# First block's projection of a two-block MLP kernel: seven products of quarters of x in chunks 1 to 3

## The chip, the core and the metric

The kernel runs on one core of a Trainium2 chip. The metric is the device time of one execution in microseconds (us), lower is better. PE is the matrix engine, DVE the vector engine, ACT the scalar engine, POOL the GpSimd engine; SP issues DMAs. The engines run at once, each working off its own queue in order, and wait for one another on semaphores.

## What is computed

Two batches of 576 tokens with 8 heads of 64 go through attention with a relative bias; the result x (1152 tokens by 512 features) goes through two blocks:

```python
h = x @ w_in                              # 512 -> 2048
g = h * clip(h + 3, 0, 6) / 6
x = g @ w_out                             # 2048 -> 512
a, b = x @ w_a, x @ w_b                   # 512 -> 1536 each
out = (a * b) @ w_out2                    # 1536 -> 512
```

The change lies in the first of these five lines and in the hand-over to the third.

## The kernel before

All matrices lie with features on the 128 partitions and tokens along the free axis. Every value is held in two parts of a shorter format, a high part (rounded) and a low part (the rest), and every product of two matrices is made as three matmuls: high by high, high by low, low by high. So each tensor that PE reads costs ACT a cast (the high part) and DVE a subtraction (the low part).

The **first block** runs in four chunks of 512 of the 2048 hidden features (`FC` = 4 tiles of 128). A chunk has two stages:

- Projection: `hidden(w, i, blk)` for 4 tiles i by 3 token blocks of 384. `proj` makes 12 matmuls (4 tiles of the 512 input features, three each) into one bank of PSUM; ACT makes relu(h+3) (L620), DVE min(.,6)*h (L621). `split_g` (L612, L613) puts the high and low parts into gh[i] and gl[i].
- Output: `out1(ch, c, w, blk)` for 4 output tiles c by 3 token blocks, 12 matmuls each over the four gh/gl, with sums over the chunks in `part` (L668 on ACT in chunk 0, L670 on DVE after).

Three pairs of PSUM banks take the groups of matmuls in turn (`bank`). In the last chunk `last_out1` weaves the first sums of the second block in between. The **second block** already uses Winograd's form of Strassen's seven products: the weight of a unit is cut into 2 by 2 quarters (A11, A12, A21, A22 with the sums S1 to S4), x into 2 by 2 quarters (two halves of the features, two halves of 576 tokens; B11, B21, B22 with the sums T1 to T4). `product` (L804) makes 12 matmuls of 288 columns for one product of one output tile, in one pair of banks; two output tiles share the weights.

**Weights** come in packed form, 68 pieces of 128x512 (`_Weights`). A piece k is loaded (three buffers `raw`, SP), `rebias` on ACT (L1014) and `join` on DVE (q = 0: L1023, q = 1: nothing, q = 2: L1027, which frees the buffer and issues the next load) restore it; `split` casts it to a slot on ACT (L1043) and takes the low part on POOL (L1044). Pieces of a unit of quarters are combined on POOL first (`combine`, L1050). `tick` and `tock` emit these steps, some joins and one slot step, between the groups of matmuls. Low parts of g wait in `later` until the next tick. The order in which the program emits the instructions is the order in each engine's queue; no scheduler changes it.

The first groups of chunk 0 are mixed with the end of the attention (L625 to L641). Then PE goes through chunk 0's output, and chunks 1, 2 and 3.

## Time and profile before

| | before |
|---|---|
| time, median of 3 runs (lowest to highest) | 583.74 us (583.36 to 584.54) |
| the profiled execution's own time | 584.19 us |
| its span | 582.4 us |
| PE / DVE / ACT / POOL busy in the span | 569.7 / 400.7 / 334.6 / 243.1 us |
| attention (PE at the first block alone from here on) | 0 to 175.1 us |
| first block, chunk 0: output from 193.9; chunks 1, 2, 3 from | 218.9, 268.9, 318.9 us |
| second block | 368.9 us to the end |

The span runs from the first to the last instruction of the profiled execution. Busy time of an engine counts the time in which at least one instruction runs. The matmul durations of the trace are longer than their spacing, since they overlap: what a stretch of PE costs is read from starts, not from durations. "Granted clock" 1.00 is PE's full 2.4 GHz; it is 1.00 in every stretch used here.

### The profile page before, as it was taken

Reading aid. Unit: us, or ns where it says so; the run is one execution under the profiler, and the core shown is the slowest. Engines: PE = TensorE matmul, PEld = TensorE weight load, DVE = VectorE, ACT = ScalarE, POOL = GpSimd, SP = SyncE. Lnnn points to the kernel's source line nnn. Section 1 sums busy time; section 2 is a strip of 40 time slices with the busy share of each in tenths; the row PEclk is TensorE's granted clock in tenths of the full one; section 3 lists DMA queues with packets and bytes.
Section 4 is the critical chain, followed back from the end, with each engine's and each line's share of the span. In section 5 each row is a group of like instructions: output and inputs, shape, how many; then the busy total and the mean of one; then the engine's idle time right before and its main releaser. Section 6 shows DMA issues by size and latency. Waiting matters only on the chain.

```text
span 582.4 us, 13871 instructions
## 1 busy us (share of the span) xinstructions
PE 569.7 (98%) x5580; PEld 508.9 (87%) x5580; DVE 400.7 (69%) x809; ACT 334.6 (57%) x661; POOL 243.1 (42%) x259
## 2 busy tenths in 40 slices
PE   8899999999999999999999999999999999999997
PEld 5267776777789999999999999999889998899986
DVE  6999999988968725865764657856752649637352
ACT  6899999987667646633640653554455543345310
POOL 0086566556844312221121532463446834367200
PEclk9999999999999999999999999999999999999999
DMA  7796877478524532443342201011271122500012
GB/s 253 225 345 165 271 215 227 117 223 191 122 66 154 166 126 73 144 145 108 110 144 73 73 0 37 1 38 43 86 248 59 37 73 72 181 2 2 1 72 92
DMA packets 29505, 69.60 MB, mean 120 GB/s; under 512 B 5888, under 2 KB 6272, under 8 KB 29440
## 3 DMA queue, kind: packets, MB, share of 16 engines
q1 hardware_dynamic: 29296, 68.61, 38.6%
q8 instruction: 44, 0.72, 0.6%
q14 instruction: 21, 0.17, 0.1%
q10 hardware_dynamic: 144, 0.09, 0.1%
HBM read 55.44 MB, written 13.25 MB: 118 GB/s over the span
## 4 chain that ended last, share of the span: by engine, by line
PE 79%; issue 7%; DVE 4%; DMA 4%; ACT 3%; POOL 1%; SPq 1%; DVEq 0%; ACTq 0%; POOLq 0%
PE pair L595 47%; PE pair L804 22%; PE sc L306 3%; PE pvb L403 3%; DMA scr<-E 2%; PE tp L347 2%; PE bps L225 2%; ACT P L323 2%; DMA bias<-scr 2%; DVE P L319 1%; DVE ht L200 1%; SPq L273 1%; PE pvb L399 1%; DMA raw<-in_wm_dram 1%; ACT PT L383 1%
## 5 line engine op out<-in xcount | busy, mean ns | idle before, releaser
L1044 POOL TENSOR_TENSOR slot<-wv,slot 128x512 fp32r<-128x512 f32 x86 | 119.5, 1395 | 219.4 <-ACT slot L1043 153.5
L595 PE MATMUL pair<-xx,slot 128*128 128x384 f32 x576 | 101.5, 335 | 0.0
L595 PEld LDWEIGHTS pair<-xx,slot 128*128 128x128 f32 x576 | 99.8, 188 | 0.2
L595 PE MATMUL pair<-gh,slot 128*128 128x384 f32 x384 | 98.6, 336 | 0.0
L804 PE MATMUL pair<-xx,slot 128*128 128x288 f32 x576 | 83.3, 296 | 0.3 <-DVE c L838 0.3
L804 PEld LDWEIGHTS pair<-xx,slot 128*128 128x128 f32 x576 | 78.6, 188 | 1.1 <-DVE c L838 0.6
L595 PEld LDWEIGHTS pair<-gh,slot 128*128 128x128 f32 x384 | 69.5, 188 | 0.0
L595 PE MATMUL pair<-slot,gh 128*128 128x512 f32 (+1 forms) x224 | 68.0, 386 | 0.0
L341 POOL TENSOR_SCALAR P<-P,st 128x576 f32<-128x576 f32 x72 | 54.7, 772 | 30.6 <-DVE st L336 14.7
L1014 ACT ACTIVATE wv<-raw 128x512 f32<-128x512 f32 x68 | 45.6, 671 | 37.6 <-DMA raw<-in_wm_dram 25.2
L595 PE MATMUL pair<-gl,slot 128*128 128x384 f32 x192 | 64.4, 336 | 0.0
L323 ACT ACTIVATE P<-P,st 128x576 f32<-128x576 f32 x72 | 55.9, 778 | 13.7 <-DVE st L319 13.3
L804 PE MATMUL pair<-tt,slot 128*128 128x288 f32 x432 | 63.5, 296 | 0.0
L1043 ACT CAST slot<-wv 128x512 fp32r<-128x512 f32 x86 | 53.1, 621 | 14.1 <-PE pair L804 6.1
L804 PEld LDWEIGHTS pair<-tt,slot 128*128 128x128 f32 x432 | 59.3, 188 | 0.2 <-ACT u L887 0.2
L620 ACT ACTIVATE t<-pair,three 128x384 f32<-128x384 f32 x48 | 28.0, 582 | 49.7 <-PE pair L595 49.7
L200 DVE TENSOR_SCALAR ht<-cs,scl,negb 128x576 f32<-128x576 f32 (+17 forms) x107 | 54.1, 543 | 0.0
L319 DVE CUSTOM_DVE_ANT_0 P<-sc,bias 128x576 f32<-128x576 f32 x72 | 51.5, 749 | 2.6 <-DMA bias<-scr 1.4
L1023 DVE TENSOR_SCALAR wm<-wv 128x512 uint32<-128x512 uint32 x59 | 40.5, 687 | 18.4 <-ACT wv L1014 18.4
L621 DVE SCALAR_TENSOR_TENSOR u<-t,pair 128x384 f32<-128x384 f32 x48 | 26.6, 554 | 38.2 <-ACT t L620 38.2
L595 PEld LDWEIGHTS pair<-slot,gh 128*128 128x128 f32 x224 | 41.4, 188 | 8.7
L595 PE MATMUL pair<-slot,gl 128*128 128x512 f32 (+1 forms) x112 | 43.0, 384 | 0.0
(118 smaller groups left out, 928.6 us busy)
## 6 DMA issues: line engine op xcount, KB each, us to landing
raw<-in_wm_dram SPq DMA_DIRECT2D x68, 512.0 KB, 3.5
scr<-E SPq DMA_DIRECT2D x36, 295.5 KB, 4.5
bias<-scr SPq DMA_DIRECT2D x17, 288.0 KB, 4.5
bias<-scr SPq DMA_DIRECT2D x17, 256.0 KB, 4.7
kraw<-in_kt_dram SPq DMA_DIRECT2D x8, 288.0 KB, 4.5
qraw<-in_qm_dram SPq DMA_DIRECT2D x8, 256.0 KB, 3.8
VM<-in_vm_dram SPq DMA_DIRECT2D x2, 1024.0 KB, 7.3
out_dram<-part SPq DMA_DIRECT2D x7, 256.0 KB, 2.0
```

The lines of the kernel that those rows point to most:

```text
L200: V.tensor_scalar(ht[:, :Dd], ltab[:, :Dd], scalar1=sc, scalar2=negb, op0=ALU.mult, op1=ALU.max)
L319: V.tensor_tensor_reduce(out=Pu, in0=sc[:, :, 0:288], in1=bt, scale=-0.125, scalar=3.0e38, op0=ALU.add, op1=ALU.min, accum_out=st[:, u : u ...
L323: A.activation(P[:, u, :], P[:, u, :], AF.Exp, bias=st[:, u : u + 1], scale=-1.0, accum_out=st[:, 2 + u : 3 + u])
L341: G.tensor_scalar(P[:, u, :], P[:, u, :], scalar1=st[:, 2 + u : 3 + u], scalar2=1.0, op0=ALU.mult, op1=ALU.mult)
L595: T.matmul(ps_ap, l, r, start=(i == 0), stop=(i == len(prods) - 1))
L620: A.activation(t, hp, AF.Relu, bias=three[:, 0:1])
L621: V.scalar_tensor_tensor(out=u, in0=t, scalar=6.0, in1=hp, op0=ALU.min, op1=ALU.mult)
L804: T.matmul(pair[:, j, 0:TQ], l, r, start=start and i == 0, stop=i == 5, skip_group_check=not start)
L1014: self.nc.scalar.activation(self.u[k], up, AF.Prelu, scale=2.0**-112, alpha=-(2.0**32))
L1023: V.tensor_scalar(mid, ub, scalar1=3, scalar2=0xFFFFFFFF, op0=ALU.logical_shift_left, op1=ALU.bitwise_and)
L1043: nc.scalar.copy(s[:, 0, :], v)
L1044: nc.gpsimd.tensor_tensor(out=s[:, 1, :], in0=v, in1=s[:, 0, :].bitcast(F32), op=ALU.subtract)
```

## The change

The projection of chunks 1 to 3 is made in quarters, as in the second block. `seven_products(ch)` replaces the twelve calls of `hidden` of a chunk: a unit is the whole chunk (its 4 tiles are two output tiles m = 0, 1 by two halves), so it has 7 products for each m, 14 in all, of 12 matmuls with 288 columns. The four pieces of weights of such a chunk are packed as quarters (last part of the diff), and POOL makes S1 to S4 from them.

The quarters B11, B21, B22 of x are parts of x itself; T1 to T4 are made once, in steps (`x_sums`, `x_steps`): one step behind each `hidden` and each `out1` of chunk 0. T2 to T4 lie in `tt`, T1 takes the place of the quarter B12 in x when chunk 0 no longer needs it. In all this is 22 instructions on DVE, 4 on POOL and 8 on ACT, all of 576 columns.

A chunk's projection then has, on DVE, 7 additions of a product and a kept sum, 8 gates (L921) and 8 low parts (L878), and on ACT 6 copies out of PSUM, 8 relus (L918) and 8 casts. The output stage of chunks 1 to 3 begins with `out1_two`: token blocks 0 and 1 of the first two output tiles run in pairs, and the tile of gh/gl that is finished last is multiplied last. In every `out1` the low part gl is now used after the two matmuls with gh. In `join_next`, `rebias(k + 1)` is emitted one step later, with the empty step q = 1.

```diff
...
+SEVEN = 1
...
+    def x_steps():
+        for _ in range(min(xrate[0], len(xsteps))):
+            xsteps.pop(0)()
...
         split_g(u, i, blk)
+        x_steps()
...
+    def x_parts(name, src, c):
+        def part(h):
+            return seven[name][h][:, c]
+
+        return (
+            lambda: A.copy(part(0), src),
+            lambda: V.tensor_tensor(out=part(1), in0=src, in1=part(0).bitcast(F32), op=ALU.subtract),
+        )
...
+    def x_sums():
+
+        def two(eng, out, a, b, op):
+            return lambda: eng.tensor_tensor(out=out, in0=a, in1=b, op=op)
+
+        minus, plus = ALU.subtract, ALU.add
+        steps = []
+        for c in range(2):
+            (h11, l11), (h12, l12), (h21, l21), (h22, l22) = (
+                [x_of(x, h, k, c).bitcast(F32) for x in (xh, xl)] for h in range(2) for k in range(2)
+            )
+            t1 = xt1[:, c]
+            (hi2, lo2), (hi3, lo3), (hi4, lo4) = (
+                x_parts(n, x, c) for n, x in (("T2", xt2), ("T3", xt3), ("T4", xt4))
+            )
+            eng = V if c else G
+            t3 = [two(eng, xt3, xt2, h11, minus), two(eng, xt3, xt3, l11, minus)]
+            t4 = [two(eng, xt4, h21, xt2, minus), two(eng, xt4, xt4, l21, plus)]
+            sums = [
+                two(V, t1, h12, h11, minus),
+                two(V, t1, t1, l12, plus),
+                two(V, t1, t1, l11, minus),
+                two(V, xt2, h22, t1, minus),
+                two(V, xt2, xt2, l22, plus),
+            ]
+            if c == 0:
+                steps += [[f] for f in sums]
+                steps[4] += t3
+                steps += [[hi2], [lo2] + t4]
+                kept = [[hi3], [lo3], [hi4], [lo4]]
+            else:
+                steps += [[f] + k for f, k in zip(sums, kept + [[]])]
+                steps += [[t3[0], hi2], [t3[1], lo2], [t4[0], hi3], [t4[1], lo3], [hi4], [lo4]]
+        for ops in steps:
+            xsteps.append(lambda ops=ops: [f() for f in ops])
...
+    seven.update({
+        "B11": (xh[:, 0:2, 0:TH], xl[:, 0:2, 0:TH]),
+        "T1": (xh[:, 0:2, TH:NTOK], xl[:, 0:2, TH:NTOK]),
+        "B21": (xh[:, 2:4, 0:TH], xl[:, 2:4, 0:TH]),
+        "B22": (xh[:, 2:4, TH:NTOK], xl[:, 2:4, TH:NTOK]),
+    })
+    for i, name in enumerate(("T2", "T3", "T4")):
+        seven[name] = (tt[:, 0, i], tt[:, 1, i])
...
-            pr += [(wh, gh[i][:, blk, :]), (wh, gl[i][:, blk, :]), (wl, gh[i][:, blk, :])]
+            pr += [(wh, gh[i][:, blk, :]), (wl, gh[i][:, blk, :]), (wh, gl[i][:, blk, :])]
...
+    def out1_two(ch, c0, ws, blk, last):
+
+        accs = [bank()[:, :TB] for _ in ws]
+        prs = [out1_products(w, blk) for w in ws]
+        seq = [0, 1, 5 - last, last]
+        for part in (seq[:2], seq[2:3], seq[3:]):
+            for acc, pr in zip(accs, prs):
+                for f in part:
+                    for i in range(3 * f, 3 * f + 3):
+                        T.matmul(acc, *pr[i], start=i == 0, stop=f == last and i == 3 * f + 2, skip_group_check=True)
+        for j, acc in enumerate(accs):
+            out1_sum(ch, c0[j], blk, acc)
+        for _ in ws:
+            tick(2)
...
+        x_steps()
...
-        for j, blk in ((0, 0), (1, 0), (0, 1), (0, 2), (1, 1), (1, 2)):
+        out1_two(ch, (0, 2), ws, 1, 2)
+        later.append(split("B11", quarter(0, 0, 0), 0))
+        for j, blk in ((0, 2), (1, 2)):
             out1(ch, 2 * j, ws[j], blk)
-            if (j, blk) == (0, 1):
-                later.append(split("B11", quarter(0, 0, 0), 0))
-            elif blk == 2 or (j, blk) == (1, 1):
+            for _ in range(1 + j):
                 next(half)
...
+    def first_gate(q, i0, c):
+        t = pw3.tile([128, 2, TQ], F32, tag="h", bufs=3, name="ht")
+        A.activation(t, c, AF.Relu, bias=three[:, 0:1])
+
+        def gate():
+            V.scalar_tensor_tensor(out=t, in0=t, scalar=6.0, in1=c, op0=ALU.min, op1=ALU.mult)
+            split_q(t, q, i0)
+
+        gates.append(gate)
+
+    def run_gate():
+        gates.pop(0)()
+        hi, lo = halves.pop(0)
+        hi()
+        later.append(lo)
+
...
+    def seven_products(ch):
+        quarters[0] = seven
+        X, X2, Y = oldest()
+        slots = {}
+
+        def use(pair, m, a, b, start):
+            if a not in slots:
+                slots[a] = ring.take((2 * FC * ch, a))
+            product(pair, slots[a], m, b, start)
+            if m == 1:
+                ring.free(slots[a])
+
+        def beat():
+
+            run_lo(len(later))
+            for _ in range(len(gates)):
+                run_gate()
+            ring.work(1, 1)
+
+        use(X, 0, "A11", "B11", True)
+        A.copy(s1, X[:, :, 0:TQ])
+        beat()
+        use(X2, 0, "S1", "T1", True)
+        beat()
+        use(X, 0, "S2", "T2", False)
+        A.copy(u2, X[:, :, 0:TQ])
+        beat()
+        use(Y, 0, "A12", "B21", True)
+        quarter_out("11", 0, 0, Y, s1)
+        use(X, 0, "S3", "T3", False)
+        A.copy(u3, X[:, :, 0:TQ])
+        beat()
+        use(Y, 1, "A11", "B11", True)
+        quarter_out("22", 0, 0, X2, u3)
+        A.copy(s1, Y[:, :, 0:TQ])
+        use(X, 0, "A22", "T4", False)
+        beat()
+        quarter_out("21", 0, 0, X, None)
+        use(X2, 0, "S4", "B22", False)
+        X, X2, Y = Y, X, X2
+        use(X, 1, "S2", "T2", False)
+        quarter_out("12", 0, 0, Y, u2)
+        run_lo(len(later))
+        A.copy(u2, X[:, :, 0:TQ])
+        run_gate()
+        ring.work(0, 1)
+        run_gate()
+        use(Y, 1, "A12", "B21", True)
+        use(X2, 1, "S1", "T1", True)
+        quarter_out("11", 1, 2, Y, s1)
+        run_lo(len(later))
+        A.copy(s1, X2[:, :, 0:TQ])
+        run_gate()
+        use(X, 1, "S3", "T3", False)
+        ring.work(0, 1)
+        c22 = pw2.tile([128, 2, TQ], F32, tag="c", bufs=3, name="c")
+        V.tensor_tensor(out=c22, in0=X[:, :, 0:TQ], in1=s1, op=ALU.add)
+        A.copy(u3, X[:, :, 0:TQ])
+        first_gate("22", 2, c22)
+        run_lo()
+        use(Y, 1, "A22", "T4", True)
+        quarter_out("21", 1, 2, Y, u3)
+        run_gate()
+        use(X2, 1, "S4", "B22", False)
+        run_gate()
+        quarter_out("12", 1, 2, X2, u2)
+        later.reverse()
+        run_lo(2)
+        run_gate()
+        order[:] = [X, Y, X2]
+        turn[0] = -1
...
+            if ch == SEVEN - 1:
+                t1_parts = [x_parts("T1", xt1[:, c], c) for c in range(2)]
+                xsteps[:] = xsteps + [part for hi_lo in zip(*t1_parts) for part in hi_lo]
+                xrate[0] = XR
+        else:
+            if ch == SEVEN:
+                while xsteps:
+                    xsteps.pop(0)()
+                for f in later:
+                    f()
+                later.clear()
+                pt1.release()
+                pt.release()
+                pw2 = tc.alloc_tile_pool(name="pw2", bufs=1, side="left", reuse_waits="tile")
+                s1, u2, u3 = (pw2.tile([128, 2, TQ], F32, name=n) for n in ("s1", "u2", "u3"))
+                pw3 = tc.alloc_tile_pool(name="pw3", bufs=1, side="left", reuse_waits="tile")
+            seven_products(ch)
...
+        for c in range(0, NC, 2):
+            ws = [ring.take(), ring.take()]
+            if ch >= SEVEN and c == 0:
+                out1_two(ch, (0, 1), ws, 0, 3)
+                out1_two(ch, (0, 1), ws, 1, 2)
+            for blk in range(2 if ch >= SEVEN and c == 0 else 0, 3):
+                for j in range(2):
+                    out1(ch, c + j, ws[j], blk, 2 if ch >= SEVEN else None)
+            ring.done(2)
...
-        if q == 0:
+        if q == 1:
             self.rebias(k + 1)
...
-        pieces += [wi[f] for f in range(f0, f0 + FC)]
+        if f0 < FC * SEVEN:
+            pieces += [wi[f] for f in range(f0, f0 + FC)]
+        else:
+            for df, h in ((0, 0), (1, 0), (1, 1), (0, 1)):
+                pieces.append(np.concatenate([wi[f + df][:, 256 * h : 256 * h + 256] for f in (f0, f0 + 2)], axis=1))
         pieces += [rows(moe_w_out, f0, c) for c in (range(NC) if f0 + FC < NF1 else (0, 2, 1, 3))]
...
```

In the order of PE's queue, at the projection of chunk 1 (xx is x with its high and low parts, tt holds T2 to T4, pair is PSUM, slot the weights), the first rows before:

```order
L595 MATMUL pair_3558<-xx,slot_2832 128x384 x12
L595 MATMUL pair_3821<-xx,slot_2832 128x384 x12
L595 MATMUL pair_3557<-xx,slot_2832 128x384 x12
L595 MATMUL pair_3558<-xx,slot_2833 128x384 x12
L595 MATMUL pair_3821<-xx,slot_2833 128x384 x12
```

and of the change:

```order
L866 MATMUL pair_3558<-xx,slot_2832 128x288 x12
L866 MATMUL pair_3830<-xx,slot_2833 128x288 x12
L866 MATMUL pair_3558<-tt,slot_2835 128x288 x12
L866 MATMUL pair_3557<-xx,slot_2834 128x288 x12
L866 MATMUL pair_3558<-tt,slot_2836 128x288 x12
```

Twelve groups of 12 matmuls with 384 columns became fourteen groups of 12 with 288.

On DVE, at the end of the projection of chunk 2 and the start of its output, in the change (c is an addition, ht a gate, gl a low part, part a sum of the output; gl_3568 and gl_3569 are tiles 2 and 3):

```order
L992 TENSOR_TENSOR c<-pair_3557,s_4194 128x576
L878 TENSOR_TENSOR gl_3568<-ht,gh_3564 128x576
L913 TENSOR_TENSOR c<-pair_3830,u_4196 128x576
L921 SCALAR_TENSOR_TENSOR ht<-ht,c 128x576 x2
L913 TENSOR_TENSOR c<-pair_3558,u_4195 128x576
L878 TENSOR_TENSOR gl_3569<-ht,gh_3565 128x576 x2
L921 SCALAR_TENSOR_TENSOR ht<-ht,c 128x576
L762 TENSOR_TENSOR part<-pair_3557,part 128x384
L762 TENSOR_TENSOR part<-pair_3830,part 128x384
L878 TENSOR_TENSOR gl_3568<-ht,gh_3564 128x576
```

where before there stood, at the end of a projection (chunk 3):

```order
L621 SCALAR_TENSOR_TENSOR u<-t,pair_3821 128x384
L613 TENSOR_TENSOR gl_3569<-u,gh_3565 128x384
L621 SCALAR_TENSOR_TENSOR u<-t,pair_3557 128x384
L613 TENSOR_TENSOR gl_3569<-u,gh_3565 128x384 x2
L670 TENSOR_TENSOR part<-pair_3558,part 128x384
```

The last quarters of the chunk now stand close together at its end, and two sums of the output stand ahead of the last low part.

On PE, at the start of the same output stage of the change (chunk 1; two accumulators in turn, tiles 0 and 1 first, tile 3 last):

```order
L743 MATMUL pair_3557<-gh_3564,slot_3580 128x384 x2
L743 MATMUL pair_3557<-gl_3568,slot_3580 128x384
L743 MATMUL pair_3830<-gh_3564,slot_2832 128x384 x2
L743 MATMUL pair_3830<-gl_3568,slot_2832 128x384
L743 MATMUL pair_3557<-gh_3565,slot_3580 128x384 x2
L743 MATMUL pair_3557<-gl_3569,slot_3580 128x384
```

Eighteen matmuls stand ahead of the first one on tile 3 (gh_3565) and twenty ahead of the first on its low part (gl_3569).

## Rows read from the trace of the kernel before

**Rows 1.** The page's parts 1 and 4: busy time; the chain by line.

```profile
PE 569.7 (98%) x5580; PEld 508.9 (87%) x5580; DVE 400.7 (69%) x809; ACT 334.6 (57%) x661; POOL 243.1 (42%) x259
...
PE pair L595 47%; PE pair L804 22%; PE sc L306 3%; PE pvb L403 3%; DMA scr<-E 2%; PE tp L347 2%; PE bps L225 2%; ACT P L323 2%; DMA bias<-scr 2%; DVE P L319 1%; DVE ht L200 1%; SPq L273 1%; PE pvb L399 1%; DMA raw<-in_wm_dram 1%; ACT PT L383 1%
```

**Rows 2.** Busy time by stage: stretch, length, then PE, PEld, DVE, ACT, POOL (instructions).

```profile
194.00:219.00 25.00, 25.00 (x146) 25.00 (x145) 10.54 (x17) 12.62 (x25) 6.22 (x5) 1.00 0.48 148
219.00:244.00 25.00, 25.00 (x146) 25.00 (x145) 17.05 (x32) 16.36 (x32) 6.47 (x5) 1.00 0.34 106
344.00:369.00 25.00, 25.00 (x146) 25.00 (x145) 19.65 (x30) 10.20 (x17) 6.38 (x5) 1.00 0.07 22
```

**Rows 3.** The same view: chunk 1's projection; the second block's first 28 products.

```profile
218.95:243.95 25.00, 25.00 (x146) 25.00 (x146) 17.00 (x32) 16.36 (x32) 6.47 (x5) 1.00 0.34 106
...
368.92:414.05 45.13, 45.13 (x337) 44.72 (x337) 29.54 (x40) 24.44 (x42) 24.56 (x17) 1.00 0.12 36
```

**Rows 4.** PE in order of time: start, us, engine, line, operation, tiles, count.

```profile
193.93 0.33 PE L595 MATMUL pair<-gh,slot 128*128 128x384 f32 x1
...
218.95 25.14 PE L595 MATMUL pair<-xx,slot 128*128 128x384 f32 x144
243.93 0.33 PE L595 MATMUL pair<-gh,slot 128*128 128x384 f32 x1
...
372.90 1.75 PE L804 MATMUL pair<-tt,slot 128*128 128x288 f32 x12
...
385.05 1.75 PE L804 MATMUL pair<-xx,slot 128*128 128x288 f32 x12
...
388.23 1.75 PE L804 MATMUL pair<-xx,slot 128*128 128x288 f32 x12
```

**Rows 5.** PE's waits from 368 us to the end: total us, times, longest.

```profile
PE pair L804 <- DVE c L838: 0.3, 1, 0.3
```

**Rows 6.** DVE by shape in the second block: count, busy us, mean ns, idle before.

```profile
L816 DVE TENSOR_TENSOR gl<-c,gh 128x576 fp32r<-128x576 f32 x24 | 23.2, 996 | 1.8 <-ACT gh L816 1.5
L1023 DVE TENSOR_SCALAR wm<-wv 128x512 uint32<-128x512 uint32 x26 | 17.9, 687 | 9.1 <-ACT wv L1014 9.1
...
L838 DVE TENSOR_TENSOR c<-c,t1p 128x576 f32<-128x576 f32 x9 | 7.5, 831 | 0.3
...
L832 DVE TENSOR_TENSOR c<-pair,s 128x576 f32<-128x576 f32 x6 | 4.5, 758 | 11.4 <-PE pair L804 11.1
```

**Rows 7.** ACT by shape: two groups of the second block, one of the first.

```profile
L816 ACT CAST gh<-c 128x576 fp32r<-128x576 f32 x24 | 16.2, 675 | 23.5 <-DVE c L838 23.2
...
L903 ACT COPY u<-pair 128x576 f32<-128x576 f32 x12 | 7.7, 640 | 14.3 <-PE pair L804 14.3
...
L620 ACT ACTIVATE t<-pair,three 128x384 f32<-128x384 f32 x37 | 21.5, 582 | 42.8 <-PE pair L595 42.8
```

**Rows 8.** DVE and POOL in order of time as the second block begins.

```profile
371.84 0.75 DVE L694 SCALAR_TENSOR_TENSOR tt<-t2p,tt 128x576 fp32r<-128x576 f32 x1
...
375.03 4.82 POOL L1050 TENSOR_TENSOR wv<-wv,wv 128x512 f32<-128x512 f32 x3
...
376.86 1.84 DVE L694 SCALAR_TENSOR_TENSOR xx<-part,xx 128x576 fp32r<-128x576 f32 x1
```

**Rows 9.** DVE in chunk 0's projection (176 to 194 us), by line; one row by time.

```profile
L613 DVE TENSOR_TENSOR gl<-u,gh 128x384 fp32r<-128x384 f32 x8 | 5.3, 661 | 0.0
L621 DVE SCALAR_TENSOR_TENSOR u<-t,pair 128x384 f32<-128x384 f32 x8 | 4.4, 554 | 2.5 <-ACT t L620 2.5
...
193.19 0.55 DVE L613 TENSOR_TENSOR gl<-u,gh 128x384 fp32r<-128x384 f32 x1
```

**Rows 10.** POOL by shape: two groups of the second block, one of the first.

```profile
L1044 POOL TENSOR_TENSOR slot<-wv,slot 128x512 fp32r<-128x512 f32 x48 | 66.4, 1393 | 77.9 <-ACT slot L1043 68.6 <-DVE wv L1027 5.2 <-PE pair L804 3.8
L1050 POOL TENSOR_TENSOR wv<-wv,wv 128x512 f32<-128x512 f32 x20 | 29.2, 1458 | 14.3 <-DVE wv L1027 13.5
...
L1044 POOL TENSOR_TENSOR slot<-wv,slot 128x512 fp32r<-128x512 f32 x29 | 38.5, 1329 | 127.9 <-ACT slot L1043 73.1 <-DVE u L621 39.0 <-DVE part L670 15.8
```

More of the change, by code (lines that the diff above doesn't have):

```diff
@@ L761, in last_out1 @@
         return half
[L763 to L791 removed]
     def product(pair, slot, m, name, start, half=(0, 1)):
[L795 removed]
+        bh, bl = quarters[0][name]
         for j in half:
@@ L819, in quarter_out @@
     def quarter_out(q, m, i0, src, add):
+        if quarters[0] is seven:
+            return first_out(q, i0, src, add)
         src = src[:, :, 0:TQ]
@@ L851, in tock @@
         halves.clear()
+    for ch in range(NCH1):
+        if ch < SEVEN:
+            for i in range(3 if ch == 0 else 0, FC):
+                w = first[i] if ch == 0 else ring.take()
+                for blk in range(3):
+                    hidden(w, i, blk)
+                ring.done()
+            if ch == SEVEN - 1:
[15 more added lines that the diff above has]
+            seven_products(ch)
+        if ch == NCH1 - 1:
+            ws = [ring.take(), ring.take()]
+            out1_two(ch, (0, 2), ws, 0, 3)
+            run_lo(len(later))
+            pw3.release()
+            pw4 = tc.alloc_tile_pool(name="pw4", bufs=1, side="left", reuse_waits="tile")
+            half = last_out1(ch, ws)
+            break
+        for c in range(0, NC, 2):
+            ws = [ring.take(), ring.take()]
+            if ch >= SEVEN and c == 0:
[5 more added lines that the diff above has]
+            ring.done(2)
+    quarters[0] = quart
+    (a11, a22), (a12, a21) = (
+        [tmp[n].rearrange("p c n -> p (c n)").rearrange("p (k j n) -> p k j n", k=2, j=2)[:, k] for k in range(2)]
+        for n in ("T1", "T2")
+    )
+    aq = {"11": a11, "12": a12, "21": a21, "22": a22}
     for ch in range(NCH2):
```

85 lines of the change are left out of this document (42 added, 43 removed).

## The prediction

> **What bounds the kernel now.** I read the page first: PE is busy in 98% of the span, and the two lines of the first and second block's matmuls hold 47% and 22% of the chain [rows 1]. So what counts is PE's own work and whatever makes it wait. The table by stage comes next: in the three stretches shown of the first block PE is busy in 25.00 of 25.00 us, while DVE has 10.5, 17.1 and 19.7 us of work and ACT 10 to 16 [rows 2]. Then PE in order of time: a projection of 144 matmuls starts at 218.95 us and the output stage behind it at 243.93, with no gap, so 24.98 us, 173.5 ns each [rows 4]. The granted clock is 1.00 there [rows 3], the higher of PE's two levels (2.4 GHz), and PE does not pause in either version for long, so I take the clock as it is. PE's time in this stage falls only if PE gets fewer columns to stream, and only as long as DVE and ACT, which must now do more in less time, stay ahead of it.
>
> **PE's work in chunks 1 to 3.** Removed are 144 matmuls of 384 columns per chunk, added 14 products of 12 matmuls with 288 columns. The price of such a product stands in the second block of the same kernel: two of them take 388.23 - 385.05 = 3.18 us, 1.59 each [rows 4], with the weights changing at every matmul as they will here. Over the first 28 products with all small waits in between it is 45.13 us, 1.61 each [rows 3], of which the trace itself names 0.3 us as a wait [rows 5]. I take 1.61, since the new stage has the same helpers around it: 14 x 1.61 = 22.56 us against 24.98, a gain of 2.42 us per chunk, **7.26 us** in three. The other end is 1.59: 22.26 us, 2.72 per chunk, 8.16 in all. Order and pairing of the output's matmuls change nothing in their number; 24 of them stay 24 x 173.5 ns.
>
> **DVE within such a projection.** Prices: an addition out of PSUM 0.76 us, a low part 1.00, a join 0.69 [rows 6]. The gate (two operands in SBUF) does not occur at this size; the nearest row is the multiplication of c with t1p, 0.83 [rows 6], I take 0.85. Before, 11 or 12 gates and low parts of 384 columns made most of the 17.0 us of DVE [rows 3]; now there are 7 x 0.76 + 8 x 0.85 + 8 x 1.00 = 20.1 us plus a join, in 22.56. On ACT 6 copies at 0.64, 8 casts at 0.675 [rows 7], 8 relus at about 0.75 (0.58 at 384 columns [rows 7], and 0.17 more as estimate for the other 192) and some seven weight steps at 0.65 give 19.8 us. Both still fit, with 10% to spare, but the work isn't spread evenly: nothing is finished before the fourth product, which ends at 4 x 1.61 = 6.44 us.
>
> From there to the thirteenth product's end (20.95 us) DVE has 5 additions, 5 gates, 5 low parts and a join, 13.7 us, for 14.5. Then comes the tail in the order that the rows of DVE above show: the addition for quarter 21 starts at about 21.15 and ends at 21.9, two gates until 23.6, the last addition until 24.35, the low part of quarter 21 until 25.35. ACT's cast for it (0.675) lies beside the last addition. PE starts the output at 22.56 and reaches this low part behind 20 matmuls, at 22.56 + 20 x 0.1735 = 26.03. So 0.7 us are left, and 0.8 us from the stretch before. The last quarter's low part is needed behind 24 + 20 matmuls, at 30.2 us; until then DVE has one low part, a gate, two sums and itself, about 4 us from 25.35. That one is covered.
>
> What can break this are the waits of DVE on ACT in the chain and POOL. The rows show what POOL can do: a low part that takes 0.75 us alone took 1.84 while three of POOL's sums ran [rows 8]. The mean of 1.00 [rows 6] already holds this, with POOL busy 95.6 of the 214 us of that block, 45%; a new chunk gives POOL 11 low parts of weights at 1.39 and 4 sums at 1.46 [rows 10], 21 us in some 47.5, 44%, so the mean should carry over. Lower end: no stall. Upper end: three more blocked operations in one chain than the mean holds, 3 x 1.09 - 1.5 = 1.8 us per chunk. I take **0.4 us per chunk**, 1.2 in all, nearer the lower end because the means leave 1.5 us of room.
>
> Here a rule bears on the sum. The Trainium skill, page "SBUF — State Buffer", section "SBUF: two separate sides", says that a DVE instruction with two inputs in SBUF and a POOL instruction exclude each other from a shared pair of ports for the whole instruction. By that rule the gate would pay like the low part, at about 1.06 as an estimate from POOL's 44% instead of my 0.85; seven of them ahead of the critical low part would eat the room and leave some 0.7 us of stall per chunk, so the time would be 579.4, still within the forecast's own range below. The row of 1.84 us agrees with the rule, the 0.83 us of the multiplication speaks for a smaller price of the gate.
>
> **The sums of x in chunk 0.** Six of the 22 DVE instructions stand ahead of the low part that chunk 0's output needs first of its last tile (tile 3, block 0), at 0.75 to 1.00 us: 4.5 to 6.0 us. DVE was idle 2.5 us while waiting for relus in this stretch [rows 9]; and the low part that started at 193.19 and ended at 193.74 [rows 9] is now needed 11 matmuls behind 193.93 [rows 4], at 195.84, so 2.1 us of lateness are free. Stall: 6.0 - 2.5 - 2.1 = 1.4 at most, 0 at least; I take **0.6 us**, below the middle, since a part of the six runs in parts of the idle time that the row does not name. The other 16 lie beside the output of chunk 0, where DVE had 10.5 of 25 us of work [rows 2]; 16 x 0.75 to 1.00 = 12 to 16 us more can just be placed. T1 is finished last, in steps behind the last outputs, and isn't needed before the second product of chunk 1. The four POOL instructions and eight casts fall on engines with 6.2 and 12.6 us of work in 25 [rows 2]. Cost 0 beyond the 0.6.
>
> **Into the second block.** There the low part of T2 ended at 372.59 [rows 8] and PE uses it in the fifth matmul from 372.90 [rows 4], 0.8 us later. DVE now brings 4 to 5 us more into the last output stage (late quarters, five more steps of joins) where it was idle 5.4 of 25 us [rows 2]. I take **0.2 us**, between 0 and 0.8.
>
> **Weights and DMA.** The number of pieces, loads and joins is the same. Shifting `rebias` by one empty step leaves two steps until its join; in the output stages DVE waits for it sometimes, but PE's next group is six banks away. POOL has until the end of the previous output to make the quarters. I cost this at nothing; what covers it is the 25 us of output stage, and if that cover went, PE would wait for a slot at a chunk's first products.
>
> **The sum.** -7.26 + 1.2 + 0.6 + 0.2 = -5.26 us. On the profiled execution's own time, 584.19 us (span 582.4), that is 578.9; this execution lies 0.45 above the median of the runs, 583.74, so I forecast **578.5 us**.
>
> **Rivals.**
> - *Nothing waits.* All stalls are hidden and products run at 1.59: 583.74 - 8.16 = 575.6 us. For it speaks that PE waited only 0.3 us in the second block [rows 5]; against it that DVE has 23 instead of 14 instructions of this size per 14 products there. Chance 0.12.
> - *The hand-over is late.* DVE reaches the last low part later by 1.2 us per chunk than PE, chunk 0 costs 1.0, the second block 0.4: 583.74 - 7.26 + 5.0 = 581.5 us, the upper part of the range. For it: only 0.7 us of room at a place that comes three times. Chance 0.17.
> - *DVE becomes the bound, and it is slower than before.* Place: the chain of 7 gates and 6 low parts from the fourth product to the hand-over. It decides once their mean passes 1.17 us: 13 x (1.17 - 0.92) = 3.3, less 1.5 of room, is 1.8 per chunk, with 1.4 and 0.8 at the other two places all of the 7.26 gone, or 1.20 with the middle costs there. At 1.29, half-way between 0.75 and 1.84 [rows 8], it would be 4.8 - 1.5 = 3.3 per chunk, 583.74 - 7.26 + 9.9 + 0.8 = 587.2 us. Against it stand 24 low parts with a mean of 0.996 [rows 6] at the same load of POOL. Chance 0.10.
> - *The gain is just given back*, or matmuls of 288 columns are not cheaper here. Against the latter stands the second block's spacing [rows 4]. Within 0.2% of 583.74: chance 0.05.
>
> **How the numbers follow.** The forecast has 0.56, with its own range of 577 to 580.5. A measurement of this kernel can tell about 0.2%, 1.2 us, from no change. Faster is the forecast and the first two rivals, 0.85; same 0.05; slower 0.10. The range runs from the first rival, 575.4, to the upper end of the second, 583.0, and leaves out the last two.
>
> **What would show it.** Right: in the changed trace the stretch from the first matmul of line 866 in chunk 1 to the first of line 743 takes 22.3 to 22.8 us, three times; the waits of PE name a low part (L878) or gate for 0 to 1 us per chunk; low parts average about 1.0 us and gates 0.85. Chunk 0's output starts at 193.9 as before, with at most 1.4 us of waiting for gl within its first 12 matmuls. Wrong: projections that take as long as 24 us with waits of PE for DVE or ACT at L866 (pair not yet read), gates above 1.17 us, or PE waiting for POOL's slots at the first products of a chunk.

## The result and the profile after

The changed kernel takes 587.45 us (median of 7 runs, 586.22 to 590.3) against 583.74 (7 runs, 581.78 to 584.54): ratio 1.0077, 95% interval 1.0051 to 1.0103, so 0.8% slower. The range of the prediction, 575.4 to 583.0, does not hold it. The two profiled executions are 586.48 us (span 584.7) and 584.19 (span 582.4).

The page's busy line and its row of the granted clock, to be read against [rows 1]: DVE has 43 us more work, POOL 39, PE only 3.4 less, and the clock is no longer full in one slice.

```profile
PE 566.3 (97%) x5652; PEld 501.3 (86%) x5652; DVE 443.6 (76%) x828; ACT 352.9 (60%) x675; POOL 281.8 (48%) x284
...
PEclk9999999999999899999999999999999999999999
```

The table by stage of the changed kernel (stretch, length, then PE, PEld, DVE, ACT, POOL with instructions, granted clock, DMA share, GB/s). Its lines are: output of chunk 0; projection and output of chunk 1, of chunk 2, of chunk 3; the first 28 products of block 2.

```profile
193.17:222.67 29.50, 27.51 (x144) 26.61 (x145) 29.43 (x35) 17.04 (x34) 19.26 (x13) 0.94 0.38 121
222.67:245.08 22.41, 22.41 (x169) 22.36 (x169) 16.63 (x23) 15.88 (x27) 6.69 (x5) 1.00 0.25 78
245.08:270.24 25.16, 25.16 (x146) 24.98 (x145) 20.63 (x35) 12.05 (x20) 13.32 (x11) 1.00 0.45 146
270.24:292.51 22.27, 22.27 (x169) 22.27 (x169) 15.02 (x20) 14.85 (x25) 6.46 (x5) 1.00 0.16 49
292.51:317.85 25.34, 25.33 (x146) 24.90 (x145) 20.37 (x34) 11.57 (x19) 13.59 (x11) 1.00 0.48 146
317.85:340.14 22.29, 22.29 (x170) 22.29 (x170) 15.04 (x20) 14.85 (x25) 6.47 (x5) 1.00 0.16 49
340.14:369.04 28.90, 26.33 (x146) 24.75 (x145) 27.24 (x38) 14.13 (x23) 13.92 (x10) 1.00 0.25 73
369.04:415.61 46.57, 45.74 (x337) 44.87 (x337) 32.20 (x41) 24.40 (x43) 25.62 (x17) 1.00 0.11 35
```

Against the kernel before ([rows 2 to 4] give its stages):

| stage | before | after | difference |
|---|---|---|---|
| up to the output of chunk 0 | 193.93 | 193.17 | -0.76 |
| output of chunk 0 | 25.02 | 29.50 | +4.48 |
| three projections | 3 x 24.98 | 22.41, 22.27, 22.29 | -7.97 |
| outputs of chunks 1 and 2 | 2 x 25.02 | 25.16, 25.34 | +0.46 |
| last output stage | 24.99 | 28.90 | +3.91 |
| first 28 products of block 2 | 45.13 | 46.57 | +1.44 |
| the rest | 168.35 | 169.09 | +0.74 |
| span | 582.4 | 584.7 | +2.3 |

The first line hides two things. The projection of chunk 0 began at 162.50 us instead of 164.09; over all the profiles of this study it begins between 162.3 and 164.9, two profiles of the changed kernel differ by 0.3 there, and no run ties the rest to the change. That is about why this pair of executions differs by 2.3 us and the medians by 3.7. And the projection took 0.8 us longer: its last 108 matmuls take 19.73 us here and 18.83 before. The sums of x begin in this stretch, and the runs below that take them out of it have 18.83 to 18.86 us again, so these 0.8 to 0.9 us are a cost of the sums too.

So the gain is there in full, and two places give it all back: chunk 0 and the last output stage with the entry of block 2. Both are full of DVE: 29.43 of 29.50 us and 27.24 of 28.90, where [rows 2] had 10.5 and 19.65 of 25.

**The first loss, chunk 0's output.** PE in order of time; the bracket is idle time and its releaser.

```profile
194.87 0.51 PE L601 MATMUL pair<-gh,slot 128*128 128x384 f32 x2
197.27 0.51 PE L601 MATMUL pair<-gl,slot 128*128 128x384 f32 x1 [1.89 <-DVE gl L620]
197.58 0.84 PE L601 MATMUL pair<-gh,slot 128*128 128x384 f32 x2
...
200.46 0.73 PE L601 MATMUL pair<-gh,slot 128*128 128x384 f32 x2
201.02 0.34 PE L601 MATMUL pair<-gl,slot 128*128 128x384 f32 x1
```

PE in stretches of 1 us there: busy, matmuls, granted clock.

```profile
197.00:198.00 1.00, 0.73 (x3) 0.76 0.00 0
198.00:199.00 1.00, 1.00 (x5) 0.50 0.14 33
199.00:200.00 1.00, 1.00 (x5) 0.50 0.79 246
```

The two matmuls at 194.87 are over for the queue at 195.22; the next starts at 197.27, a pause of 2.05 us. Then the granted clock is 0.50 (1.2 GHz): 12 matmuls take 201.02 - 197.27 = 3.75 us instead of 12 x 0.1735 = 2.08. That is 1.67 us more, so 3.72 of the 4.48.

What made that low part late, on DVE and POOL by time:

```profile
178.01 1.85 DVE L652 TENSOR_TENSOR xt<-xx 128x576 f32<-128x576 f32 x1
190.51 1.55 DVE L620 TENSOR_TENSOR gl<-u,gh 128x384 fp32r<-128x384 f32 x1
194.29 1.25 DVE L646 TENSOR_TENSOR tt<-xt,tt 128x576 fp32r<-128x576 f32 x1
194.89 1.92 POOL L652 TENSOR_TENSOR xt<-xx,xt 128x576 f32<-128x576 f32 x1
195.93 1.29 DVE L620 TENSOR_TENSOR gl<-u,gh 128x384 fp32r<-128x384 f32 x1
```

The last row is the one that PE waits for. It began at 193.19 in the kernel before [rows 9]. Ahead of it stand the sums of x (L652, L646), and it takes 1.29 us instead of 0.55, lying beside a sum of x on POOL. The row of 1.55 us at 190.51 lies beside the first sums on POOL as well (190.20 to 193.35).

**The second loss, the last output stage.** PE's waits, total, times, longest: L601 is this stage; L866 is block 2, where the wait of 1.3 us stands ahead of the first product, so at the end of the 28.90 us.

```profile
PE pair L866 <- DVE part L762: 1.3, 1, 1.3
PE pair L601 <- DVE part L762: 1.3, 2, 0.7
PE pair L866 <- DVE xx L787: 0.5, 1, 0.5
```

DVE by time; instructions of these lines take about 0.75 us where no POOL instruction runs, and each of these four stands beside one (POOL has 13.92 us of work here, 6.4 in [rows 2]).

```profile
356.36 1.84 DVE L792 TENSOR_TENSOR t2p<-part,t1p 128x576 f32<-128x576 f32 x1
359.93 1.84 DVE L787 SCALAR_TENSOR_TENSOR tt<-t2p,tt 128x576 fp32r<-128x576 f32 x1
365.92 1.84 DVE L787 SCALAR_TENSOR_TENSOR xx<-part,xx 128x576 fp32r<-128x576 f32 x1
371.63 1.85 DVE L787 SCALAR_TENSOR_TENSOR xx<-part,xx 128x576 fp32r<-128x576 f32 x1
```

### The profile page after: what moved, and what is told of

Its sections match the earlier page's. It is cut to its first block, busy times and chain, and to the rows that moved or that the text cites. A ratio compares the mean times of both kernels' runs of the same rounds, so it can differ in the third digit from the quotient of the medians.

```text
span 584.7 us, 14062 instructions
## 1 busy us (share of the span) xinstructions
PE 566.3 (97%) x5652; PEld 501.3 (86%) x5652; DVE 443.6 (76%) x828; ACT 352.9 (60%) x675; POOL 281.8 (48%) x284
## 5 line engine op out<-in xcount | busy, mean ns | idle before, releaser
L1263 POOL TENSOR_TENSOR slot<-wv,slot 128x512 fp32r<-128x512 f32 x95 | 136.2, 1441 | 183.6 <-ACT slot L1262 162.4
L866 PE MATMUL pair<-xx,slot 128*128 128x288 f32 x864 | 125.0, 296 | 2.6 <-DVE part L762 1.3
L866 PEld LDWEIGHTS pair<-xx,slot 128*128 128x128 f32 x864 | 117.9, 188 | 4.2 <-issue 1.6
L866 PE MATMUL pair<-tt,slot 128*128 128x288 f32 x648 | 94.8, 296 | 0.3 <-DVE tt L787 0.3
L866 PEld LDWEIGHTS pair<-tt,slot 128*128 128x128 f32 x648 | 88.8, 188 | 0.7 <-DVE tt L787 0.5
L601 PE MATMUL pair<-gh,slot 128*128 128x384 f32 x288 | 75.2, 342 | 1.4 <-DVE part L762 1.3
L601 PE MATMUL pair<-slot,gh 128*128 128x512 f32 (+1 forms) x224 | 68.0, 386 | 0.0
L1269 POOL TENSOR_TENSOR wv<-wv,wv 128x512 f32<-128x512 f32 x36 | 51.1, 1420 | 10.9 <-DVE wv L1244 9.5
L601 PEld LDWEIGHTS pair<-gh,slot 128*128 128x128 f32 x288 | 52.7, 191 | 3.2 <-DVE part L762 2.2
L601 PE MATMUL pair<-gl,slot 128*128 128x384 f32 x144 | 49.1, 341 | 1.9 <-DVE gl L620 1.9
L601 PEld LDWEIGHTS pair<-slot,gh 128*128 128x128 f32 x224 | 41.4, 188 | 8.9
L601 PE MATMUL pair<-slot,gl 128*128 128x512 f32 (+1 forms) x112 | 43.1, 385 | 0.0
L1244 DVE SCALAR_TENSOR_TENSOR wv<-raw,wm 128x512 uint32<-128x512 uint32 x59 | 40.2, 681 | 1.6
L405 PE MATMUL pvb<-PT,VM 128*32 128x128 f32 (+1 forms) x1280 | 39.3, 263 | 2.0 <-DVE PT L387 0.7
L405 PEld LDWEIGHTS pvb<-PT,VM 128*32 128x32 f32 x1280 | 32.0, 110 | 6.0 <-issue 3.6
```

Source lines behind the costliest of these rows:

```text
L405: T.matmul(pvb[32 * w : 32 * w + 32, p, c0:c1], VM[:, k, b * H + 2 * p + u, d], PT[:, 4 * u + k, c0:c1], start=False, stop=(k == 3),)
L601: T.matmul(ps_ap, l, r, start=(i == 0), stop=(i == len(prods) - 1))
L866: T.matmul(pair[:, j, 0:TQ], l, r, start=start and i == 0, stop=i == 5, skip_group_check=not start)
L1263: nc.gpsimd.tensor_tensor(out=s[:, 1, :], in0=v, in1=s[:, 0, :].bitcast(F32), op=ALU.subtract)
L1269: self.nc.gpsimd.tensor_tensor(out=self.v[to], in0=self.v[a], in1=self.v[b], op=op)
```

## The experiments

Theory A: the stages themselves work as predicted, and the loss is DVE's work in two places, the sums of x in chunk 0 and the joins with their POOL work in the last output stage. Rivals: B, the new order of the weight steps (rebias); C, the late quarters or chunk 0's lateness make the last stage long; D, DVE's count of instructions alone matters, not what POOL does beside it (the text of that run calls the opposite theory L). Every ratio is to the kernel before, in runs on the same chip.

### Without the sums of x

```diff
-    x_sums()
...
-        seven[name] = (tt[:, 0, i], tt[:, 1, i])
+        seven[name] = seven[like]
```

> The changed kernel without the sums of x: no x step runs, T1 stands for the quarter B12 and T2, T3, T4 for B11, B21, B22 themselves, so the four sums are left out of the result. Theory A (the sums crowd DVE in chunk 0 and put the low part of tile 3 late): the output of chunk 0 goes from 29.50 back to 25.0 to 25.3 us, the granted clock stays 1.00 there, no wait at L601 for gl; time 587.45 - 4.3 = 583.1 us, same or slightly below the kernel before. Rival B (the order of the weight steps, with rebias one step later, keeps DVE waiting): the wait for gl stays over 1 us and the time stays above 586. The last output stage (28.90 us) and the entry into block 2 are the same under both.

Measured: 581.59 us, ratio 0.9971 (0.9954 to 0.9988): faster than the kernel before, by 0.3%, with the sums left out of its result. Chunk 0's output:

```profile
191.79:216.81 25.02, 25.02 (x145) 25.02 (x145) 12.11 (x18) 12.80 (x25) 12.04 (x9) 1.00 0.46 151
```

No wait, full clock, 25.02 us. The last output stage stays at 28.88. So the first loss is the sums', all of it, and the second is another matter. The fall of the ratio from 1.0077 to 0.9971 is 6.2 us, more than the 4.5 of chunk 0's output in the profile. Of the rest, 0.9 us is the projection of chunk 0 (18.83 us here, 19.73 there); the next experiment bears on what remains.

### The changed kernel again

> The changed kernel once more, unchanged, for the spread of its times (586.22 to 590.3 us). Theory A': DVE's lateness in chunk 0 reaches PE on two ways, through the low part gl of tile 3 (1.9 us) and through ACT, whose copies of the output wait behind a cast of a sum of x (2.0 and 2.7 us in the profiles of two variants); the second is there in some executions, and the granted clock falls behind one pause or the other. Then the median is 587 to 588.5 us again with a spread of 3 to 4 us, and the output of chunk 0 takes 29 to 30 us in a profile with one pause and 31 to 32 in one with both. Rival: the spread has nothing to do with chunk 0; its output takes 29.5 us whatever the time.

587.15 us (586.31 to 589.32, 6 runs), ratio 1.0068 (1.0048 to 1.0088). Its profiled execution (586.52 us) has one pause, and 29.48 us in chunk 0's output. The runs without joins and with chunks 1 and 2 (both below) do the same up to the output of chunk 1 and give the other case, 31.41 and 31.42 us. PE and ACT of the run without joins, by time:

```profile
210.18 0.34 PE L601 MATMUL pair<-gl,slot 128*128 128x384 f32 x1
212.52 0.93 PE L601 MATMUL pair<-gh,slot 128*128 128x384 f32 x2 [2.00 <-ACT part L760]
...
210.35 0.67 ACT L645 CAST tt<-xt 128x576 fp32r<-128x576 f32 x1 [5.71 <-DVE xt L652]
...
212.01 0.46 ACT L760 COPY part<-pair 128x384 f32<-128x384 f32 x1
```

The cast of a sum of x that DVE had not made stood at the head of ACT's queue for 5.71 us; the copy out of PSUM stood behind it, and PE had no free bank. In this execution the clock stayed at 1.00 after the first pause (2.08 us) and fell after this second one. So DVE's lateness reaches PE by two ways, and the same work loses 4.5 or 6.4 us. Which of the two goes with the clock: in both profiles of the changed kernel it fell behind the first pause, PE came to this bank later for it and lost only 0.3 us there; in the three profiles where it did not fall (without joins, chunks 1 and 2, and rebias back, below) the second pause was 2.2, 2.2 and 2.8 us, and the clock fell behind that. That the spread of 3 to 4 us between runs comes from this alone is likely but not shown, since the unprofiled executions have no rows.

### All sums in the output of chunk 0

```diff
-XR = 1
+XR = 2
...
         split_g(u, i, blk)
-        x_steps()
```

> The changed kernel with no x step in the projection of chunk 0; all 22 come with the output of chunk 0, two per call. Theory A in its form 'it is the amount of work' (DVE has no idle time left from 190 to 224 us): the wait for gl at the head of chunk 0's output and the fall of the clock go (4.2 us), but the sums end later and PE waits 3 to 6 us at the second product of chunk 1, which reads T1; time 586 to 589 us. Theory A in its form 'it is the place' (six steps stand ahead of one low part): no new wait over 1 us, time 583.0 to 584.0 us.

590.2 us, ratio 1.0117 (1.0092 to 1.0143), above the 586 to 589 expected. The wait for gl is gone, but in three waits PE loses 3.5 us to ACT's copies, the clock falls behind the longest of them, chunk 0's output takes 32.15 us with DVE busy in 31.36, and the projection of chunk 1 takes 23.79 instead of 22.41. So the place of six steps alone is not the cause; the 22 are too much work for this stretch. The wait came a few microseconds earlier than expected, through ACT.

### The sums of POOL on DVE

```diff
-            eng = V if c else G
+            eng = V
```

> The changed kernel with the four sums of x that POOL makes (T3 and T4 of the first 128 features) on DVE, at the same steps. Theory L (a POOL sum holds up DVE's instructions that read two SBUF operands: the low part of 1.29 us at 195.93 lies beside one): DVE gets 4 x 0.74 = 3.0 us more work, but its low parts of g in chunk 0 fall from a mean of 0.87 us towards 0.62 and the sums of x from 1.0 towards 0.75, so the output of chunk 0 takes no longer than in the changed kernel, 27 to 29.5 us, and the time is 585 to 587.5 us. Rival D (DVE's own count of instructions is all that matters): 3 us more in chunk 0's output, time 590 us.

588.03 us, ratio 1.0093 (1.0074 to 1.0113), above the 585 to 587.5 of theory L and below the 590 of rival D. Chunk 0's output takes 28.16 us, but that is no gain: part of the loss has moved into the projection ahead of it. PE's two longest waits, the first in the projection:

```profile
193.27 2.37 PE L601 MATMUL pair<-xx,slot 128*128 128x384 f32 x12 [2.12 <-DVE u L628]
...
198.92 0.44 PE L601 MATMUL pair<-gl,slot 128*128 128x384 f32 x1 [1.38 <-DVE gl L620]
```

From PE's last run of 108 matmuls in the projection to the start of chunk 1, chunk 0 takes 50.13 us here, 49.23 in the changed kernel and 43.85 before. The clock stays at 1.00 all the way here, so PE's pauses alone are some 2.6 us longer than in the changed kernel, which lost 1.7 to the clock. Low parts of g and sums of x on DVE from 170 to 222 us, first in the changed kernel (count, busy us, mean ns):

```profile
L620 DVE TENSOR_TENSOR gl<-u,gh 128x384 fp32r<-128x384 f32 x12 | 10.4, 866 | 0.0
L652 DVE TENSOR_TENSOR xt<-xt,xx 128x576 f32<-128x576 f32 x9 | 9.0, 998 | 0.0
L646 DVE TENSOR_TENSOR tt<-xt,tt 128x576 fp32r<-128x576 f32 x6 | 7.8, 1293 | 0.0
```

and with all sums on DVE:

```profile
L652 DVE TENSOR_TENSOR xt<-xt,xx 128x576 f32<-128x576 f32 x12 | 12.2, 1013 | 0.1
L620 DVE TENSOR_TENSOR gl<-u,gh 128x384 fp32r<-128x384 f32 x12 | 8.5, 709 | 0.0
```

The low parts of g fall from 0.87 to 0.71, 1.9 us in all. The sums of x get little shorter (their mean over all forms goes from 1.14 to 1.06 us), since POOL still has the weights. DVE's whole queue shows the balance: it reaches the last part of T1 50.83 us behind the start of that PE run instead of 49.87, so 3.0 us more work delayed DVE by 1.0 us. On DVE, then, D's count falls and a sum on POOL is about two thirds as dear as one on DVE itself. For the time nothing is settled: PE's pauses grew by nearly as much as D says, and the time did not, because the clock did not fall.

### Rebias back at its old step

```diff
-        if q == 1:
+        if q == 0:
             self.rebias(k + 1)
```

> The changed kernel with rebias back at the step q = 0, as in the kernel before. Theory A: this step has no part in the loss, 587.4 us within 0.7. Rival B: DVE's waits for rebias go and the time falls by 1 to 3 us.

589.97 us, ratio 1.0114 (1.0084 to 1.0143). Nothing is gained, so rival B falls. Theory A's 587.4 within 0.7 is missed too; whether the step makes it worse than the changed kernel stays open: the intervals overlap, and its profile has both pauses in chunk 0 (31.97 us).

### No joins in the last output stage

```diff
-            out1_two(ch, (0, 2), ws, 0, 3)
+            out1_two(ch, (0, 2), ws, 0, 3, 0)
...
-            ring.work(1, 1)
+            ring.work(2 if ch == NCH1 - 1 else 1, 1)
```

> The changed kernel with no joins emitted in the last output stage of the first block; the last chunk's projection emits two steps of joins per beat instead of one. Theory A (the seven half-joins of 0.69 us, 4.8 us, and the POOL work that they release fill DVE there): the last output stage goes from 28.90 to 25.0 to 26.0 us, the first 28 products of block 2 from 46.57 to 45.1 to 45.5, time 587.45 - 4.4 = 583.0 us. Rival C (the late gates and low parts of the projection that run into this stage are what is too much): the stage stays over 27.5 us and the time falls by less than 1.5 us. If the weights of block 2 then come too late, PE waits for a slot at its first products instead.

604.19 us, ratio 1.0352 (1.0324 to 1.0381), where theory A had 583.0. As a cure it fails, since block 2 then lacks weights: it takes 233.4 us instead of 215.7, with 9.9 us of waits for slots and clock falls behind them. As a measurement of the last output stage it serves: 26.68 us, between the 25.0 to 26.0 of theory A and the 27.5 of rival C. The stage, then DVE by time:

```profile
341.97:368.65 26.68, 25.41 (x146) 24.96 (x145) 22.83 (x30) 11.90 (x19) 14.42 (x10) 1.00 0.00 1
...
350.08 1.09 DVE L762 TENSOR_TENSOR part<-pair,part 128x384 f32<-128x384 f32 x2 [2.16 <-PE pair L743]
...
355.94 1.85 DVE L792 TENSOR_TENSOR t2p<-part,t1p 128x576 f32<-128x576 f32 x1
359.53 1.84 DVE L787 SCALAR_TENSOR_TENSOR tt<-t2p,tt 128x576 fp32r<-128x576 f32 x1
...
365.54 1.84 DVE L787 SCALAR_TENSOR_TENSOR xx<-part,xx 128x576 fp32r<-128x576 f32 x1
```

The joins are worth 28.90 - 26.68 = 2.2 of the 3.9 us. The late quarters are worth nothing: DVE stands idle 2.16 us behind them. What is left, one wait of 1.3 us at the entry of block 2 and the waits behind it, stands behind the same three instructions held up by POOL, 1.1 us each. Of these the kernel before has only the second, at 359.86. That POOL's work makes the rest is argued from these rows; no run took it away. A rival stands beside it: the new order of this stage (`out1_two`), which every run with seven products in chunk 3 has. It too shows in the rows, since the order puts one sum more (0.7 us, at 355.28) between the sixth and the seventh sum of `part` than before. No run has the new order alone.

### Other sets of chunks

```diff
-SEVEN = 1
+SEVEN = (2,)
...
-        if ch < SEVEN:
+        if ch not in SEVEN:
...
-        x_steps()
+        x_steps() if turns else None
```

The set is (2,), (1, 2) or (2, 3); where chunk 3 is not in it, its projection and the last output stage are as before the change. In the sets (2,) and (1, 2) chunk 3 reads T1 in the place of B12, which T1 has overwritten. The last line stands in the sets without chunk 1 (no step in the projection of chunk 0).

> Seven products in chunks 1 and 2; chunk 3 and the last output stage as in the kernel before; the sums of x as in the changed kernel, crowded into chunk 0. Theory A: twice the gain of 2.4 us less the loss of chunk 0, which was 4.5 us in the profile of the changed kernel and 6.4 and 6.9 in the profiles of two variants: 583.7 - 4.8 + (4.5 to 7) = 583.4 to 585.9 us; the last output stage is back at 25.0 us and the first 28 products of block 2 at 45.1. Rival C (the last stage's loss comes from chunk 0's lateness, handed on through the weights): last stage over 27 us here too.

Chunks 1 and 2: 585.99 us, ratio 1.0053 (1.0037 to 1.007), 0.1 above theory A's range. Chunk 0's output 31.42 us, last output stage 24.96.

> Seven products in chunks 2 and 3 with the changed kernel's last output stage; the sums of x spread from the output of chunk 0 to that of chunk 1. Theory A: chunk 0's output 25.0 us, no fall of the clock; gains 2.4 and 2.7 us, losses of the last output stage 3.9, of the entry into block 2 1.4 and of a wait in it 0.6: 583.7 + 0.8 = 584.5, between 583.8 and 585.3 us. If the last stage recovers with the lateness of chunk 0 (rival C): 579 to 580 us.

Chunks 2 and 3: 587.92 us, ratio 1.0082 (1.0056 to 1.0108), more than expected. Chunk 0's output 25.02 us, last output stage 28.93. Together these two tell the losses apart: each stands with its own stage, whatever the other does, and C falls in its second form too. The 3.4 us too many are in chunk 1's projection, 28.63 us instead of 24.98: the sums of x now lie there, PE pauses 2.0 us, and the clock falls behind that.

> Seven products in chunk 2 alone; chunks 1 and 3 and the last output stage as in the kernel before; the sums of x run one per call from the output of chunk 0 to the output of chunk 1, some 70 us, and none in the projection of chunk 0. Theory A (the losses lie in the crowded chunk 0 and in the last output stage alone): the gain of one chunk is left, 49.98 - 47.6 = 2.4 us, time 583.7 - 2.4 = 581.3, between 580.8 and 582.0 us; chunk 0's output 25.0, chunk 2's projection 22.3 us. Rival: each such chunk costs more than its own stage shows (later weights, later x sums), time 583 to 585 us.

Chunk 2 alone: 582.78 us, ratio 0.9997 (0.9971 to 1.0023), neither theory's number. The projection of chunk 2 has its 22.3 us; chunk 1's takes 27.25 instead of 25.0. PE and DVE by time:

```profile
233.97 6.35 PE L601 MATMUL pair<-xx,slot 128*128 128x384 f32 x34 [1.81 <-DVE u L631]
...
229.48 5.11 POOL L1273 TENSOR_TENSOR wv<-wv,wv 128x512 f32<-128x512 f32 x3
...
231.63 1.82 DVE L649 TENSOR_TENSOR tt<-xt,tt 128x576 fp32r<-128x576 f32 x1
```

Three sums of weights on POOL hold up the sums of x and low parts on DVE, and the gate that frees PE's bank (L631, at 233.38) stands behind them.

> Seven products in chunk 2 alone; the sums of x run with the output of chunk 0, the first three calls of chunk 1's projection and the output of chunk 1, none beside POOL's three sums of weights in chunk 1's projection. T1 takes the place of B12 as in the changed kernel, so chunk 3, made plainly here, reads T1 for B12. Theory A: PE's wait of 1.8 us in chunk 1's projection (sums in chunk 2 alone, steps at every call: 27.25 us) goes, that stage takes 25.0 us; 582.78 - 2.2 = 580.6, between 580.0 and 581.5 us, and faster than the kernel before by 0.3 to 0.5%. Rival: the same work is then late at the entry of chunk 2 (T1 or T4), 582 us or more.

The edit adds `and i == 0` to the last line of the diff. 580.99 us, ratio 0.9968 (0.9949 to 0.9987), faster. Chunk 0's output, chunk 1's projection, chunk 2's projection, last output stage:

```profile
192.87:217.88 25.01, 25.01 (x145) 25.01 (x145) 22.02 (x30) 14.12 (x28) 14.17 (x9) 1.00 0.44 143
217.88:242.87 24.99, 24.99 (x146) 24.99 (x146) 21.11 (x37) 18.30 (x35) 11.82 (x8) 1.00 0.35 111
...
267.88:290.17 22.29, 22.29 (x169) 22.29 (x169) 15.02 (x20) 14.88 (x25) 6.46 (x5) 1.00 0.07 25
340.50:365.51 25.01, 25.01 (x145) 25.01 (x145) 19.56 (x30) 10.19 (x17) 6.29 (x5) 1.00 0.07 23
```

All stages as theory A has them: no PE pause with DVE at 21 to 22 of 25 us. This kernel still leaves B12 out of chunk 3, which reads T1 there; the next two put it back.

### A version that beats both

```diff
-        "T1": (xh[:, 0:2, TH:NTOK], xl[:, 0:2, TH:NTOK]),
+        "T1": (own, None),
...
-    ring.add(pw, 0, 6, NSLOT - 5)
+    ring.add(pw, 0, 5, NSLOT - 5)
```

> The same order with a place of its own for T1, so that chunk 3 reads B12: for the space one buffer of weights fewer (9 for 10), two buffers instead of three for c and for the gate, and T4 made in the place of T2. Theory A, if the buffers suffice: 580.6 us, between 580.0 and 581.8, faster than both kernels. If the fewer buffers make the gates wait for one another or the weights late, chunk 2's projection takes over 23 us or later stages stretch, 582 to 585 us.

584.3 us, ratio 1.002 (1.0005 to 1.0034), in the range of the second case. Chunk 2's projection is fine (22.32 us), so two buffers for c and the gate suffice; block 2 is 216.27 us long instead of 213.4, with ACT and DVE waits of PE that the tenth buffer had kept away.

```diff
+                pv_ = tc.alloc_tile_pool(name="pv_", bufs=1, side="left", reuse_waits="tile")
+                ring.add(pv_, 0, 1, 0)
```

> Seven products in chunk 2 alone with T1 in a place of its own and the sums of x spread, as in the run before it (584.3 us), but the tenth buffer of weights comes back from chunk 3 on, where that space is free again. The run without it lost 2.8 us in block 2 (366.53 to 582.8, 216.3 us, against 213.4) and 0.5 in the output of chunk 2. Theory: block 2 needs the tenth buffer; it is back at 213.4 to 213.8 us, time 581.0 to 582.0, faster than the kernel before by 0.2 to 0.35%. Rival: the pieces are already behind when the buffer comes back, or the two buffers for c and the gate cost the rest; 583 to 584 us.

581.3 us (12 runs, 580.19 to 583.9), ratio 0.9966 (0.9951 to 0.998): faster than the kernel before by 0.34%. Block 2 is back at 213.35 us.

## Why the prediction was wrong

- **PE's gain: right.** 7.26 us forecast, 8.16 as upper end, 7.97 measured: a projection takes 22.3 to 22.4 us, products 1.59 to 1.60 instead of 1.61. (ACT has 7 copies in it, not the 6 that the description and the sum count; 0.64 us, and PE did not wait for it.)
- **Hand-over: right in sign, too dear.** 1.2 us forecast in three chunks; within the projections PE does not wait at all, and the outputs of chunks 1 and 2 are 0.46 us longer. The gate had no row before. In the changed trace, up to 365 us (gates with c, low parts):

```profile
L921 DVE SCALAR_TENSOR_TENSOR ht<-ht,c 128x576 f32<-128x576 f32 x21 | 16.0, 760 | 3.8 <-ACT ht L918 3.4
...
L878 DVE TENSOR_TENSOR gl<-ht,gh 128x576 fp32r<-128x576 f32 x24 | 22.9, 973 | 0.5
```

  0.76 instead of the 0.85 taken, and 0.97 against the 1.00 taken. The Trainium skill (page "SBUF — State Buffer", section "SBUF: two separate sides") would have the gate excluded by POOL like the low part, the estimate for it was 1.06. No run here puts that to the test: POOL is busy 29% of a projection, and none of the 24 gates lies beside it for more than 0.2 us.
- **The sums of x in chunk 0: the step that failed.** Taken at 0.6 us, at most 1.4; measured 4.48 and 6.4, and 0.9 more in the projection. The six instructions ahead were priced at 4.5 to 6.0 us and took 6.08, and the needed low part was due where the prediction put it. But by 6.0 less 2.5 of idle time it should have ended at most 3.5 us later; counted from the start of PE's last 108 matmuls in the projection, it ended 5.1 later (23.78 instead of 18.64). What the sum lacks is the price of the other low parts: the eight of that stretch, the needed one included, took 7.57 us instead of 5.27, 2.3 more, of which the two beside POOL's sums make 1.7. The four POOL sums were costed at nothing because POOL had 6.2 us of work in 25. By the Trainium skill's rule of the shared ports (the same section) this was to be expected, and the row of 1.84 us in [rows 8] showed it; I used it for the projections only. Giving POOL's sums to DVE did not save the stage either, so their place is not all of it. "12 to 16 us more can just be placed" failed too, and by its own sum: 10.5 + 16 is 26.5 us in a stage of 25. DVE had no idle time left, and ACT's copies stood behind its casts.
- **"I take the clock as it is": failed.** It rested on there being no long pause; behind a pause of 2.05 us the granted clock was 0.50, which cost another 1.67 us.
- **Into the second block: failed.** Taken at 0.2 us, at most 0.8; measured 3.91 + 1.44. I counted late quarters and five steps of joins against 5.4 us of idle time. The quarters cost nothing, the joins 2.2; POOL's doubled work in this stage and the new order of its sums I had not counted. How the rest divides between these two stays open.
- **Weights, DMA, rebias: right** at nothing.
- **The rival that came out.** "DVE becomes the bound" gave 587.2 us, next to the 587.45 measured, but by another mechanism: it put the loss into the chain of gates and low parts, at a mean over 1.17 us, and that chain ran at 0.76 and 0.97 without a wait. The agreement of the numbers is chance. Its chance of 0.10 was too low because I tested it only where the gain is made. (The range, too, is not what the sums give: its lower end is printed as 575.4 where the first rival has 575.6, and nothing in the text yields the 583.0.)

## What to carry to other kernels

When PE is saved columns by sums on DVE, add up DVE's work per stage with POOL's beside it: in these stages PE ran without a pause with DVE up to 22.3 of 25 us busy, and lost time wherever DVE was full. The busy share alone does not tell: the last output stage without joins lost 1.7 us with DVE at 22.8 of 26.7, because one chain of sums was late. Work that is made once must be spread over time in which nobody waits for it; here spreading it over some 75 us ahead of its first use, and using the seven products in one chunk instead of three, turned 0.8% slower into 0.34% faster. Price a new helper instruction at its duration beside the other engine, and follow every queue it stands in, ACT's casts included.
